# Decay attention with a two-of-four expert layer: multiplications and six gate operations from VectorE to GpSimd, in a new order

## The chip, the core and the metric

The kernel runs on one core of a Trainium2 chip. The metric is the device time of one execution in microseconds (us). A core has TensorE (PE, with its weight loads listed apart as PEld), VectorE (DVE), ScalarE (ACT), GpSimd (POOL) and the DMA queue of SyncE (SP). Each works through its own list of instructions in order, and semaphores tie the lists together.

## What is computed

Eight batches of 576 positions with 8 heads of 64 columns go through causal attention with a decay, and the result, turned to 576 x 512, through four attention "experts", of which each position takes the two with the largest gate logits:

```python
scores = scale * q @ k.T + cum[:, None] - cum[None, :]      # cum: running sum of log f, per head
attn   = softmax(where(causal, -1e9, scores)) @ v           # per batch and head
x      = attn.transpose(0, 2, 1, 3).reshape(B, S, H * D)
logits = x @ w_gate                                         # two of four experts per position
for e in range(E):
    a   = softmax(where(causal, -1e9, scale * (x @ wq[e]) @ (x @ wk[e]).T))
    ye  = a @ (x @ wv[e]) @ wo[e]
    out += gate[e] * ye                                     # gate: softmax of the two, else 0
```

## The kernel before

**Units.** Work is cut into pairs of heads. A batch has four pairs of kind "a" (attention) and two of kind "m" (experts): a3.2 is pair 2 of batch 3, m3.1 the second expert pair of batch 3. Each pair goes through `prep_attn` or `prep_moe` (the q and k operands, each split into a rounded part and a remainder), `max_pass` (row maxima, reduced by VectorE, L624 and L640), `scores` (score matmuls L716 and L717, exponentials on ScalarE, the triangular cuts L703 and L772 on GpSimd, and on GpSimd the additions L776, L778, L780 and L782 that fold a pair's blocks into `R` for the row sums), and `attend` (28 matmuls with the values, L801, and two copies of the output to `ot`).

**Row sums.** Two pairs share the rest. `row_sums` multiplies `R` with ones on TensorE (`sm`, L839), turns the sums (L854), takes reciprocals (for experts times the gates, L862), turns them back (L868) and spreads them over the partitions with two DMAs (`bt`, L874). `apply_rows` then takes each of the two pairs in turn: the output is multiplied by the spread reciprocals (L886, 128 x 576), ScalarE writes the rounded part (L905), and VectorE the remainder (L913). The rounded parts and remainders of a batch's four attention pairs are the operands of `moe_front` (values and gate logits, L439) and `prep_moe` (L544); those of its two expert pairs are the operands of `project_out` (`po`, L936), whose blocks go to the output.

**Gates.** After a batch's values, `moe_front` makes the gates from the logits in fifteen small operations on 80, 20 or 5 columns (L473 to L505), all of them on VectorE but one exponential on ScalarE (L494). 256 short matmuls in all, 32 for a batch, turn the gates (`pg`, L512), and two copies put them where `row_sums` of the expert pairs reads them.

**The order.** Every function is a generator which yields after each step. `ORDER` is a string in which two characters name a task; the kernel calls the next step of that task at each place. So the order of each engine's list is written out by hand in this string, and `SLOTS` names the buffer that each new tile takes. `NWARM` = 110 matmuls on zeros (L205) are one of the tasks, for the beginning.

Of the kernel before, what the change touches and what calls it, by code (L numbers as in the profile page):

```python
# [32 lines left out]
0e0e0e0e4z0e080303080h080e0e0e080808080h08080808080h08080h0e080e0e0j0j0j0o0t040e0j0j0j0e0e080808080808084w4w080e
0j0j0o0o0j0j0j0j0j0j0j0j0j0j0j0j0j0j0j0j0e0j0o0h0f0f0f0f0o0f0f0o0o0q0f09080j0t0j090f0f080f0f0f0f03080q0A0q0f0q0q
0q0j0j0q0f0f0f0f0q0q0t0q0k0k0k0A0q0k0q0d0f0f0q0k0t0k0k0k0a0t0t0k0a0a0a0a0f0q0F040k0k0k0q0k0q0k0f0k0q0q0f0k0q0i0k
0k0q0q4A0q0q0q0k0k0k0k0k0f0q0v0v0v0v0v0v0f0v0v0v0v0p0v0A0k0q0A0a0A0F0a0g0v0v0v0v0v0v4A0v0v0g0t0k0q0o0v0l0v0q0l0a
0q0q0B0t4y0a090C0C0v0v0v0v0v0C0g0C0C0C0C0C0C0C0C0r0r0r0r0r0r0r0r0b0f0r0r0r0r0r0C0C0C0r0v0v0v0v0C0C0C0r0r0r0r0C0C
# [1006 lines left out]
```

## Time and profile before

| | us |
|---|---|
| median of 3 runs (641.13 to 643.39) | 641.9 |
| profiled execution | 642.41 |
| span of the profiled execution | 640.7 |
| TensorE busy | 627.2 (98%) |
| VectorE busy | 541.1 (84%) |
| ScalarE busy | 481.9 (75%) |
| GpSimd busy | 409.7 (64%) |
| DMA: mean over 16 engines | 43.7% of the span |

Busy time counts an engine while an instruction runs, a VectorE instruction that stands still behind another engine included. Idle time of an engine matters only where TensorE ends up waiting for it. The granted TensorE clock is 1.00 of its full level, 2.4 GHz, in every stretch of the span but the last 0.7 us, which holds no work.

### The profile page before, as it was taken

What the parts mean: (1) busy time and instruction counts of PE and PEld (TensorE: products, weight loads), DVE (VectorE), ACT (ScalarE), POOL (GpSimd) and SP (SyncE); (2) the same over time, 40 slices, a digit from 0 to 9 for tenths busy, and PEclk for the clock granted to TensorE, in tenths of its full rate; (3) what the DMA queues carried; (4) which work ended last, traced back from release to release, by engine and by line L of the source; (5) the groups of instructions that cost most, each with busy time, mean ns of one, the idle gap of its engine ahead of it and who ended that gap; (6) DMA issues with size and microseconds to landing.
All of it is one profiled execution on the core that took longest, in us unless ns stands there. A gap on an engine that the chain in (4) does not pass through costs nothing.

```text
span 640.7 us, 15170 instructions
## 1 busy us (share of the span) xinstructions
PE 627.2 (98%) x5303; PEld 538.1 (84%) x5303; DVE 541.1 (84%) x1541; ACT 481.9 (75%) x1057; POOL 409.7 (64%) x519
## 2 busy tenths in 40 slices
PE   8899999999999999989999999999999999999997
PEld 6677889789888988869888898887987789879976
...
GB/s 195 154 168 194 136 55 143 137 90 96 141 140 130 80 158 144 161 55 62 170 145 66 148 174 40 139 142 83 119 105 136 134 109 76 79 98 21 107 70 202
DMA packets 33531, 76.90 MB, mean 120 GB/s; under 512 B 4395, under 2 KB 4875, under 8 KB 33455
## 3 DMA queue, kind: packets, MB, share of 16 engines
q1 hardware_dynamic: 33455, 75.94, 43.7%
...
## 4 chain that ended last, share of the span: by engine, by line
PE 88%; DVE 6%; issue 2%; DMA 2%; ACT 1%; SPq 1%; POOL 0%; DVEq 0%; POOLq 0%
PE pp_m L544 16%; PE ob_a L801 10%; PE pv L439 7%; PE po L936 7%; PE s_a L716 7%; PE s_a L717 7%; PE m_a L618 6%; PE m_m L618 4%; PE ob_m L801 4%; PE oa_a L801 4%; PE s_m L716 4%; PE s_m L717 4%; PE sm_a L839 3%; PE warm L205 2%; PE oa_m L801 1%
## 5 line engine op out<-in xcount | busy, mean ns | idle before, releaser
L703 POOL TENSOR_SCALAR_AFFINE_SELECT P_a<-P_a 128x256 f32<-128x256 f32 x128 | 65.3, 527 | 112.7 <-ACT P_a L734 67.2
L716 PE MATMUL s_a<-ka_a 128*128 128x320 f32 (+4 forms) x384 | 104.2, 296 | 1.1 <-DVE mxs_a L624 0.9
L717 PE MATMUL s_a<-kq 128*128 128x320 f32 (+4 forms) x384 | 102.9, 294 | 0.0
L624 DVE CUSTOM_DVE_ANT_0 junk_a<-m_a,mask 128x192 bf16<-128x192 f32 (+2 forms) x186 | 86.8, 486 | 17.3 <-PE m_a L618 15.4
L618 PE MATMUL m_a<-kq 128*128 128x448 f32 (+3 forms) x372 | 80.7, 304 | 4.0 <-DVE mxs_a L624 3.1
L552 ACT ACTIVATE kq<-pp_m 64x288 fp32r<-64x288 f32 x128 | 51.9, 406 | 31.6 <-PE pp_m L544 30.1
L716 PEld LDWEIGHTS s_a<-ka_a 128*128 128x128 f32 (+1 forms) x384 | 69.2, 180 | 4.4 <-DVE mxs_a L624 1.6
L717 PEld LDWEIGHTS s_a<-kq 128*128 128x128 f32 (+1 forms) x384 | 68.6, 180 | 1.2
L557 DVE TENSOR_TENSOR ka_m<-pp_m,kq 64x288 fp32r<-64x288 f32 x128 | 58.2, 454 | 12.9 <-ACT kq L552 9.7
L801 PE MATMUL ob_a<-P_a,va 128*64 128x320 f32 (+1 forms) x512 | 67.5, 406 | 0.0
L776 POOL TENSOR_TENSOR R_a<-P_a 128x896 f32<-128x896 f32 x32 | 67.5, 2110 | 0.1
L618 PEld LDWEIGHTS m_a<-kq 128*128 128x128 f32 (+1 forms) x372 | 57.6, 180 | 9.7 <-DVE mxs_a L624 4.4
L703 POOL TENSOR_SCALAR_AFFINE_SELECT P_m<-P_m 128x256 f32<-128x256 f32 x64 | 33.7, 543 | 48.2 <-ACT P_m L734 31.0
L778 POOL TENSOR_TENSOR R_a<-R_a,P_a 128x640 f32<-128x640 f32 x32 | 55.3, 1731 | 1.8
L801 PEld LDWEIGHTS ob_a<-P_a,va 128*64 128x64 f32 x512 | 35.8, 137 | 24.0
L716 PE MATMUL s_m<-ka_m 128*128 128x192 f32 (+2 forms) x192 | 51.8, 295 | 0.0
L717 PE MATMUL s_m<-kq 128*128 128x192 f32 (+2 forms) x192 | 50.9, 294 | 0.0
L624 DVE CUSTOM_DVE_ANT_0 junk_m<-m_m,mask 128x192 bf16<-128x192 f32 (+2 forms) x96 | 44.9, 485 | 5.3 <-PE m_m L618 4.3
L399 DVE TENSOR_TENSOR ka_a<-xin_a,ka_a 64x1152 fp32r<-64x1152 f32 x32 | 47.9, 1497 | 0.7
L734 ACT ACTIVATE P_a<-s_a 128x512 f32<-128x512 f32 x64 | 36.8, 598 | 13.2 <-PE s_a L717 12.0
L399 DVE TENSOR_TENSOR ka_a<-xin_a,kq 64x1152 fp32r<-64x1152 f32 x29 | 42.5, 1465 | 0.8
L618 PE MATMUL m_m<-kq 128*128 128x320 f32 (+3 forms) x192 | 41.2, 298 | 0.0
...
## 6 DMA issues: line engine op xcount, KB each, us to landing
...
```

What stands on the lines that cost most here:

```text
L399: eng.tensor_tensor(lo, x[at], hi.bitcast(F32), ALU.subtract)
L544: nc.tensor.matmul(pp[:, :HS], w[:, c, es], x[c][:, gs], start=(n == 0), stop=(n == 3 * KC - 1))
L552: nc.scalar.activation(hv[h], src[h], AF.Copy)
L557: nc.vector.tensor_tensor(lo[:, h, gs], src[h], hv[h].bitcast(F32), ALU.subtract)
L618: nc.tensor.matmul(dst, qB[0:K, h, i0 : i0 + dst.shape[0]], kB[0:K, h, j0:j1], start=True, stop=True)
L624: nc.vector.tensor_tensor_reduce(jk[:, :n], src, mask[:, MW - n :], 1.0, init, ALU.add, ALU.max, acc)
L703: return nc.gpsimd.affine_select(pv, pv, [[0, 2], [1, 128]], ALU.is_ge, 0.0, base=0, channel_multiplier=-1)
L716: nc.tensor.matmul(dst, kaf[:, c : c + m], qA[:, h, i0:i1], start=True, stop=False)
L717: nc.tensor.matmul(dst, kqf[0:K, c + h * S : c + h * S + m], qB[0:K, h, i0:i1], start=False, stop=True)
L776: g.tensor_tensor(r[:, :, 128:S], p[:, :, 320:768], p[:, :, 768:1216], ALU.add)
L778: g.tensor_tensor(r[:, :, 256:S], r[:, :, 256:S], p[:, :, 1216:1536], ALU.add)
L801: mm = nc.tensor.matmul(dst[64 * h : 64 * h + 64, c0 : c0 + rhs.shape[-1]], vs[h][0:kp, blk], rhs, start=first, stop=last,)
```

## The change

Two things are moved from VectorE to GpSimd: the multiplication by the reciprocals in `apply_rows` (48 of them), and six of the gate operations of each batch (48 in all). The sums, comparisons, maxima and reciprocals of the gates stay on VectorE. No instruction is added or left out, and no DMA.

```diff
 (moe_front)
-        nc.vector.tensor_tensor(g4, g4, up.unsqueeze(1).to_broadcast([128, 5, E, E]), ALU.mult)
+        nc.gpsimd.tensor_tensor(g4, g4, up.unsqueeze(1).to_broadcast([128, 5, E, E]), ALU.mult)
...
-        nc.vector.tensor_tensor(t4, t4, low.unsqueeze(1).to_broadcast([128, 5, E, E]), ALU.mult)
+        nc.gpsimd.tensor_tensor(t4, t4, low.unsqueeze(1).to_broadcast([128, 5, E, E]), ALU.mult)
...
-        nc.vector.tensor_tensor(g4, g4, t4, ALU.add)
+        nc.gpsimd.tensor_tensor(g4, g4, t4, ALU.add)
...
-        nc.vector.tensor_tensor(gt, lg, mx.unsqueeze(2).to_broadcast([128, 5, E]), ALU.subtract)
+        nc.gpsimd.tensor_tensor(gt, lg, mx.unsqueeze(2).to_broadcast([128, 5, E]), ALU.subtract)
...
-        nc.vector.tensor_tensor(gt, gt, wins, ALU.mult)
+        nc.gpsimd.tensor_tensor(gt, gt, wins, ALU.mult)
...
-        nc.vector.tensor_tensor(gt, gt, sm.unsqueeze(2).to_broadcast([128, 5, E]), ALU.mult)
+        nc.gpsimd.tensor_tensor(gt, gt, sm.unsqueeze(2).to_broadcast([128, 5, E]), ALU.mult)
 (apply_rows)
-            nc.vector.tensor_tensor(xf, grp["bt"][p], xf, ALU.mult)
+            nc.gpsimd.tensor_tensor(xf, grp["bt"][p], xf, ALU.mult)
```

The string `ORDER` is written anew from end to end, and five of the `SLOTS` lines with it (P, wide, banks, strips and some of the small ones); both orders have 4939 places and call the same steps. Three stretches of the two strings, read step by step:

- The beginning: of the 110 warm-up matmuls 85 stand ahead of the first matmul of the second maximum pass (a0.1) in the old order, 99 in the new one.
- Row sums to use: between the `sm` matmuls of a0.3 and the first matmul on rows that they scale stand 77 matmuls in the old order and 80 in the new; for a7.3 it is 91 and 101.
- The end: in both orders TensorE's list runs attend m7.0, attend m6.1, `sm` of m7.1, `pg` of batch 7, attend m7.1, and then 30 `po` matmuls ahead of the first `po` of batch 7. In the new order GpSimd's list ends with L776 to L782 of m7.1, L496 and L505 of batch 7, and the multiplications of batches 6 and 7.

## Rows read from the trace of the kernel before

**Rows 1.** The page's busy time, share of the span and instructions, by engine.

```profile
PE 627.2 (98%) x5303; PEld 538.1 (84%) x5303; DVE 541.1 (84%) x1541; ACT 481.9 (75%) x1057; POOL 409.7 (64%) x519
```

**Rows 2.** Stretches of 20 us: length, engines' busy us (instructions), clock, DMA share, GB/s.

```profile
0.00:20.00 20.00, 16.31 (x119) 12.97 (x119) 14.15 (x35) 15.47 (x19) 18.23 (x30) 1.00 0.59 192
20.00:40.00 20.00, 17.65 (x130) 14.13 (x128) 17.86 (x56) 17.09 (x31) 19.16 (x20) 1.00 0.55 159
...
260.00:280.00 20.00, 19.45 (x147) 16.08 (x145) 17.88 (x43) 17.26 (x37) 11.00 (x16) 1.00 0.54 152
280.00:300.00 20.00, 18.20 (x165) 16.64 (x166) 16.70 (x49) 12.75 (x30) 9.30 (x14) 1.00 0.21 61
...
420.00:440.00 20.00, 18.95 (x147) 15.43 (x144) 17.38 (x43) 17.21 (x40) 12.88 (x18) 1.00 0.51 149
...
sum 640.70, PE 627.20 PEld 538.14 DVE 541.12 ACT 481.87 POOL 409.68; mean PE 19.01 PEld 16.31 DVE 16.40 ACT 14.60 POOL 12.41
```

**Rows 3.** Timeline of 274 to 284 us: start, us, engine, instruction [idle before].

```profile
274.39 2.10 POOL L776 TENSOR_TENSOR R_m<-P_m 128x896 f32<-128x896 f32 x1
274.57 2.54 DVE L913 TENSOR_TENSOR xl_a<-ot_a,xh_a 128x576 fp32r<-128x576 f32 x1
...
276.57 1.94 POOL L778 TENSOR_TENSOR R_m<-R_m,P_m 128x640 f32<-128x640 f32 x1
277.04 2.09 DVE L886 TENSOR_TENSOR ot_a<-bt_a,ot_a 128x576 f32<-128x576 f32 x1
...
279.96 2.11 POOL L776 TENSOR_TENSOR R_m<-P_m 128x896 f32<-128x896 f32 x1
...
280.53 2.15 DVE L913 TENSOR_TENSOR xl_a<-ot_a,xh_a 128x576 fp32r<-128x576 f32 x1
280.66 0.39 PE L618 MATMUL m_a<-kq 128*128 128x256 f32 x1 [1.06 <-DVE mxs_a L624]
...
283.42 1.03 PE L618 MATMUL m_a<-kq 128*128 128x448 f32 x6 [1.14 <-DVE mxs_a L624]
```

**Rows 4.** Timeline of VectorE and GpSimd about 430 us.

```profile
430.15 3.83 DVE L886 TENSOR_TENSOR ot_a<-bt_a,ot_a 128x576 f32<-128x576 f32 x2 [0.47 <-DMA bt_a<-rr_a]
...
431.21 2.10 POOL L776 TENSOR_TENSOR R_m<-P_m 128x896 f32<-128x896 f32 x1
```

**Rows 5.** VectorE's groups by line: busy us, mean ns | idle before.

```profile
L886 DVE TENSOR_TENSOR ot_a<-bt_a,ot_a 128x576 f32<-128x576 f32 x32 | 28.9, 906 | 0.9 <-DMA bt_a<-rr_a 0.8
...
L886 DVE TENSOR_TENSOR ot_m<-bt_m,ot_m 128x576 f32<-128x576 f32 x16 | 12.1, 754 | 0.5 <-DMA bt_m<-rr_m 0.5
...
L505 DVE TENSOR_TENSOR gt<-gt,sm 128x20 f32<-128x20 f32 x8 | 3.2, 398 | 0.2
...
L479 DVE TENSOR_TENSOR t<-t,low 128x80 f32<-128x80 f32 x8 | 1.8, 225 | 0.0
```

**Rows 6.** One line each of GpSimd: least/median/longest ns, first to last start.

```profile
L778 POOL TENSOR_TENSOR R_a<-R_a,P_a x32: 1548/1568/2753, 30.4 to 560.7; 128x640 f32<-128x640 f32 x32
...
L780 POOL TENSOR_TENSOR R_a<-R_a,P_a x32: 995/1012/2166, 33.1 to 562.4; 128x384 f32<-128x384 f32 x32
...
L782 POOL TENSOR_TENSOR R_a<-R_a,pl x32: 447/454/1652, 47.3 to 563.5; 64x128 f32<-64x128 f32 x32
```

**Rows 7.** GpSimd's longest wait: who waited for whom, us in total, times, longest.

```profile
POOL P_a L703 <- ACT P_a L734: 67.2, 18, 9.1
```

**Rows 8.** Timeline of the end; the last row is from the chain that ended last.

```profile
617.46 0.45 POOL L782 TENSOR_TENSOR R_m<-R_m,pl 64x128 f32<-64x128 f32 x1
...
618.23 1.18 PE L839 MATMUL sm_m<-R_m,ones_col 128*32 128x288 f32 x16
...
625.73 0.76 DVE L886 TENSOR_TENSOR ot_m<-bt_m,ot_m 128x576 f32<-128x576 f32 x1 [0.50 <-DMA bt_m<-rr_m]
...
627.98 0.75 DVE L886 TENSOR_TENSOR ot_m<-bt_m,ot_m 128x576 f32<-128x576 f32 x1
...
622.53 14.52 PE po L936 x63
```

More of the change, by code (lines that the diff above doesn't have):

```diff
@@ L33 @@
[L33 to L37, printed above, removed]
@@ new lines @@
+4w4w4w4w4w4w4w4w01004w4w0000004w0202024z4w0c024w4w4w000202020202024w4w4w4w024w05054w0505020202020202024w4w02024w
+4w4z4w024z02020c0c024w020202024z070707030702020207074w054w4w0c0c07030307074w0705054y0c070c0707070707070707070707
+0h4w4w030303030e030303030303030303034w4z4z03030303030307070d07070e0e0707070h4z4z0h0e0e0e0h0e0e0e0e0e040e0c0e0c0e
+0e0e0e0e0e0e030h0e08080808080308080o080e0e08080h0e08080808080h080t08080e08080808080j0j0j0j0j0j0j0j0e030j0e0e0e0e
+4y044w0j4w0j4w4w0i0j0j0o0j0j0j0j0j0j0j0j0j0j0j0f0f0o0t090o0h090j0f0j0j0f0f0f0j0o0o0v0A0o0f0f080q0f0f0j080q0f0j0q
@@ new lines @@
+0q0f0q0f0f0q0q0f0f0f0f0t0f0q0q0q0q0f0f0k080q0q0q0q0k0k0q0f0q0q0q0q0q0f090q0q0q0k0k0k0k0k0a0k0t0t0A0a0a0k0q040k0k
+0k0k0k0k0k0k0q0q0t0a0p0k0k0k0k0k0F0A0v0v0A0f0a0a0k0v0v0v0v0v0A0C0k0v0v0v0a0F0g0v0f0v0v0v0v0v0v0v0v0v0v0q0v0q0q0g
+0k0o0f0l0l0t0v0C0C0C0C0C0v0C0C0t0g0r0r0r4A0r0r0r0r0r0r0r0C0a0a0C0r0r0r0v0v0v0r0b0r0C0C0C0C0C0C0C0C4A0r0C0C0C0r0r
+4A0F0m0m0m0m0r0m0b0v0v0r0r0C0w0m0m0C0l0F0C0w0w0w0w0w0r0b0F0b0m0b0b0b0b0w0A0b0w0w0w0w0s0w0m0s0s0M0C0H0b0n0H0w0w0w
+0w0w0H0H0H0H0H0w0H0C0C0H0N0H0H0M0C0R0R0N0n0C0n0R0n0H0H0n0n0n0n0H0u0w0n0H4y0O0H0H0N0M0H0H4A0R0H0H0H0H0N4A0w0w0H0r
@@ new lines @@
+0M0Y0A0R0H0r0N0H0r0r4A0A0N0C0N0N0N0N0N0N0N0N0N0N0N0N0N0N0N0N0N0N0w0M0N0N0N0N0N0N0N0N0N0N0D0D0D0D0D0D0D0D0D0D0D0D
+0D0N0N0O0M0O0O0D0D0D0D0D0F0H0H0F0F0H0O0D0D0x0I0I0D0G0x0Y0O0H0O0Y0O0O0O0M0M0D0M0M0M0x0n0Y0N0O0O0O0O0O0O0O0O0O0O0O
+0O0O0w0I0n0Y0I0I0w0w0I0w0I0I0I0I0I0I0O0O0I0Y0I0I0I0I0I0Y0y0Y0y0R0O0O0+0O0N0O0O0D0R0R0R0R0R0R0R0R0R0R0R0R0R0R0R0R
+0R0+0+0R0R0+0R0+0y0D0+180I0R0D0I0D0R0R0M0R0R0R0R0I0R0I0I0y0y0P0P0P0P0P0P0+0+0+0+0+0P0P0P0P0P0R0M0S0P0S0S0S0S0S0S
+0S0S0y0M0P0P0P0S0S110M0M0M0I0y0P0P0P0P0P0B0S0M0M0M0P0P0b0S0S0y0I0S0S0M0S110S110S0S0S0S0S0S0M0M0M0M0M0P0P0S0z0M0S
@@ new lines @@
+0R0R0R0+0+0+0+0+0M0M0M0M0M0M0+0+0+0+0S0I0M0J0+0+0+0M0S0z0J0E0E0E0K0+0S0K0K180+0+0M0K0y0T0P0S0T0T0T0T0T0T0T0T0T0T
+0T0T0T0T0T0T0T111111110+0K0+0T0T0T1313131d0Z0K0P0+13131313131313130+180Q0K181813120-0-1313131d0-0Q131313130K0J0-
+0T13130K130T0T0-130T0-13130-0-0-0-0-0-0-0-130Q0-180-0-0-0-0M131a1a0-0-1a1a1a1d1d1a0-1a130M181a1a1a0M0M0M0L0M0U13
+1a0M0z13111d0M0M0M0L100z1a0L0z101a0z0L0L0L0U0L1a1a1a1a1a1e1a1a1a1a0U14101f0z1414141414141414141f140z1a1a1a1a1f14
+0T141f1f1f141f1f1f1f141f141414141414140V0z0M0L0L1a1f1f1f1f1f1a1a0M0M1a141k0V0V1w0V1k1k1l1f1f1l1l181l1l1l1b1b1b1b
@@ new lines @@
+1414191b1b1b0L1d0-1b1b0V1f1f1f1f1f0V0L1f1f1d1p1p1p1p1k1k1p1b1b1b0V1b1b1b1b0V0V1b1b1b1b1b1b4A0V1f1l1l1f0-1m0-1f0z
+0z1l1l1l1l1l1l1l1l1l1p1f1l1l1l1l1l1l1l1l1l1l1l1l1l1l1d1p1p1B0-1b1p1b1p1p1p1p1p1p1p1p1p1l1l1k1k1k1k1k1k1q141l0W1l
+1m1m1p1l1m1p1p1p1m1m1p1p1p1g1p1m1p1p1p1p1p1p1p1m1q1p161m160W161m1m0W0W1g0W0W1g4A0W1q1f1g1g1g1g1q1q1p1q1q1q1q1k1k
+1k1k1k1k1k1p1g1q1q1p1b1g1g1g1g4A4A1g1g4A1m1m1m1m1m0W1m1m1m1q1q161q1g1g1g1g1g1g1m1m1g1g1g1g1g1l1l1m161q1q1q1q161m
+1m1m1I1w161k1q1w1w1w1w1w1B1w1q151c151h161h1p1m1m1m1q1h17151k1k1k1q0W1q1q1q1k1k1k171y1k1k1y1y1q1y1y1m1m1c1y1y1y1n
@@ new lines @@
+1y4A171q1k1k1g171q1b1n1n1n1n1y1y1k1n1n1n1n1n1n1n1n1k1n1n1n1x161k1C1y1y1y1y1y1y1y1n1y1y1n1i1717171n1n1n1B1y1y1y1y
+1k1y1n1i1i1i1q1i1r1q1r1r1r1r1r1r1r1r1r1r1r1r1r1r1r1r1r1r1r1r1r1B1B1B1N1B1i1k1k1r1r1r1i1i1i1D1y1o1y1J1D1r1D1D1D1D
+1o171I1I1I1n1D1o1D1D1D1D0X0X0X0X0X1k1D1D1k1D1N1y1k1k1y1I1D1D1D1D1D1D1D1D0X0X0X0X0X0X1B1y1D1D1D1D1k1k1n1s1D1k1D1k
+1K1c1k1D1K1K1z1z1z1z1z1z1z1k1k1s1s1K1K1K1K1z1z1z1z1K1K1D1K1E1E1z1z1n1K1z1z1z171U1z1z1K1K1K1V1K1K1K1K1z1K1K1E1n1P
+171K1t1t1t1k1N1N1N1j1V1E1j1j1j1V1k1K1K1K1j1j1j1j1j1E1U1U1E1E1V1E1E1K1K1E1E1E1E1k1U1t1t1E1E1E1E1E1K1U1K1U1K1K1E1V
@@ new lines @@
+1V2g1W1z1Z1I1Z1V1z1I1P1P1P1P1V1V1V1V1V1V1P1P1z1z1E1E1Z1I0X1Z0X1P1P1V1V1P1V1V1V1Z1z1z1Z1U1U1U1U1U1L1V1Z1L1L1L1L0X
+0X1P1N1P1P1V1t1P1V1P1N1E1L1L1L1L1L1E1V1P1P1P1P1P1P1P1P1P1P241t1L1V1V1V1V1E1V1V1V1V1V1V1V1V1V1V1P1z1L1L1L1L1L171L
+1E1E1L1P1t1P1L1L1L1Z1Z1+1L241U1U1U1t1Z1u1U1U1U1U1W1W1Z1W1W1W1W1W1W1P1P1W1U1Z1W1Z1Z1Z1Z1Z1Z1Z1Z1Z1Z1V1W1W1W1j1j1W
+1t1L1Z1Z1Z1Z1Z1Z1Z1Z1Z1Z1Z1Z1W1L1Z1Z1+1G1G1L1N1G1G1G1G1Z1Z1A1G1G1A0W0W1A1O1F1u1u1G1u1u1u1u1u1u1F1W1Q1Q1Q1Q1Q1W1Q
+1F291+1+1+1+1+1Q1Q1Q1Q1+1Q1+1+1Q1+1W1Q1Q1H1Q1Q1Q1Q1Q1Q1Q1W1W1V1Q1+241+1W1W1W1L1Q1W1H1+1+1W1+1+1+1+1U1U1U1U1U1U1U
@@ new lines @@
+1U1U1Q1Q1Q1u1u1U1U1+1+1+1+1W1+1W1W1U1+1+1U1U241H1H251W1R1M1H1H1H1H1S1S1S1R1+1X1R1X1X1X261+1H1S1M241+261S261X261S
+26261U1U1X1X1X1X1X1X1X1X1X1X1X261X1X2626261X1X1X261X1S1-1-1-1+1-2h1S2l1-1H29291v1v241M2429291v261v1v1v1v1v1v1v1v
+1v1X261X26262626261v1v1v2626261-1-1-1-1-1-26261-1-1S1T1U1U241U1U1v1v1-2a1-2626261v1-1U1-2b2b2b2b1v2b2b2b291T2b2b
+2b1X1-1-1-1-1U262g262b1-1Y1Y2g1v2l201Y1-1-2029262b2b262b2b2b1T2s2g2g1-2b27272727272b272027271X1T2i2b2b2b2b1T1T2b
+1-2b2b2b2727272i2i27272727271U1U1U1U1U27271T2b2t2b21211U211U2i2t2i2g2s2s2i2i2l1U292t2t2b1T2b2c2c2c2c2c1T2c2c2c2c
@@ new lines @@
+2c212l1T2c2c2c2c2c2c2c2s2c272c1T2l2s27271H2i272l2l2s2s2s2s2s2i2i2s2s2s2n27212n21212i2n2n2n2n2n2s2s2s2s2n2n2n2n1v
+2i212s2s2s2s2s2s2s2c4y4y2i2t2i272c2c2c2c2s212i2i2i212s2i2s2n2n2t2t2t2t2E2t2n2n2n2n2n2i2i2n2n2t2t2s2n2n2n2n2n2n2t
+2t2t2t2i2i2i2i2i2t2t2t2t272c272i2t2t2t2t2t2t2t2t2t2t2t2t2i2i2i2i2t2t2t2n2n28282n222g2t222c2n2l2x222g22222222222d
+2m2t2e2o2e2e2d2o282e2j2j2e2s2s2s2s2s2u2u2u2s2s2o2e2e2j2j2j2j2u2o2o2s2u2o2o2u2u2u2o2o2s2u2j2j2j2j2u2u2s2j2j2j2j2j
+2s2e2o2o2o2u2u2u2t2u2s2s2s2o2u2o2o2o2o2j2u2j2u2u2222222u2u2f2s2y2o2d2j2j2E2j2o2J2o2o2E2E2j2o2u2j2u2E2o2o2x2E2E2e
@@ new lines @@
+2u2j2u2o2o2j2x2j2x2x2x2x2x2x2x2x2x2x2x2x2x2x2x2x2x2x2x2x2x2x2x2x2x2x2x2x2x2x2x2x2x2s2y2s2f2k2u2u2u2u2u2k2y2y2y2y
+2y2f2f2f2k2J2y2y2E2y2p2y2y2F2y2y2y2y2y2y2y2y2y2v2f2G2G2v2v2y2y2y2j2K2G2G2v2v2v2v2v2v2y2y2v2v2v2f2G2v2G2G2G2G2G2G
+2v2v2v2v2v2v2v2v2v2v2y2p232G2G2G2G2x2x2G2G2y232G2G2G2G2f2J2q2q232G2f2G2Q2q2q2Q2y2z2z2y2z2z2z2z2z2z2z2G2z2z2z2z2z
+2z2q2z2z2z2z2z2z2z2z2z2G2G2z2G2G2Q2w2v2L2v2w2S232J2J2J2J2L2L2L2L2L2L2L2J2L2L2q2s2G2H2H2p2323232G2L2q2L2H2L2L2L2L
+2L2L2L2H2L2L2L2L2L2Q2Q2V2q2q2H23232L2L2w2S2S2z2S2S2S2H2H2S2S2H2H232S2S2H2H2H2S232Q2H2H2H2H2H2v2H2H2H2H2L2L2L2S2L
@@ new lines @@
+23232S2S23232r2S2S2S2S2X2S2S2S2S2A2V2V2S2r2r2r2V2V2B2s2A2A2V2s2B2B2B2B2r2r2r2r2r2r2M31302M2S2M2M2M2M2M2M2M2M2S2H
+2H2M2M2M302M2M2M2M2M2M2H2S2S2Q2X2X2X2X2X2X2X2X2s2X3h2H2Q313131323131312X2B3131313030312X2X30302B312M2M3c2X2X2X31
+312M2M312M2M2M3131313131313131312X2X2X2X312B2X3131313131312S2S2S2X2X2X2X2X3130303131313031303030303030303132312T
+2T2T2T2T3032322T302V2H2T2T2T2T2T2T2T2T2T2T2T2V303030302B2B3232323232322T2T2C2C30302C2C2C2C2X2O2X2X2X2C2C3c3c2O2O
+2f2O3c3c2O3o2O322N3c3c3c2I2I2I2R2O2N2N2O2Y2Y2Y2Y3232323232323232322T0X2T3e32352T2T2Y2Y2Y2T2Y32322Y35352Y353e2Y2W
@@ new lines @@
+2Y2Y3e3e322Y2Y352Y2Y2Y2Y2Y2Y2Y2Y3232322Y3e3e32323e3e3e3e3e2C3h35353535353535353535353535353535353535353535353535
+3535352f322C2r3e2C3e3e3e2P3e2D30303e3e3030303030302D2D303033333335353535333333333333332P2T3333363636333333363636
+363636353333363e3333333e3e3e3e2U3e2O3h362D36333o3h3e2Y3e363636362Y332T3636363636363636363h2+2D2+342U2+2+3e2+3336
+363e2Z36362P362+2+2+2U343334372Z2P373j2P2P2P3j3j3h3e2P2P3e2Z37373j3j3j3j3030303030373737373737373j3j3j3j2D2P3t37
+3737303737303h3j3j2-3j3j3j3j3j3j30373j37372+37373o3737303030303h2D2-2P3j3j3j3o3f3f3f3f3f3f3f3o3f3f372D3j383j2-3j
@@ new lines @@
+373t3j383j2-2D2D2D2D3q383q3q3q3q3q3q3q3q3f3f3f3f3f2D2-3q3q3A3A3A3f3f3f3q3q3q3q3q3j3q3q3j3q3f3f33333739392-303030
+3t39392-3q3q3k3q3k2-3k3k3k3k3k2-3q3q3k3k3k2-3v3k3k3k3k3A3A3q3q3B39393t3t3t3k3k3k3k3A393q3k3k3k3p3B3q3q3B3o3o3o3B
+3B3B3q3v3v3v3f3f3f3f3B3B3F3F3B3B3v3v3v3v3v3v3v3A3A3A3B3B3B3B3k3k3B3M3B3B3B3B3B3B3B3B3B3r3r3B3B3B3B3B3B3B3r3r3r3r
+3B3B3B3B2-3v3v3v3v3v3d393A3A3A3F3F3F3r3C3r3r3r3C3r3r3r3v3k3v3v3v3v3v3v3v39393A3A3v3A3A3v3r3f3r3r3r3r4y3v3k3k3F3r
+3r3C3C3C3C3A3A3F3F3v3v3G3f3f3t3t3C3C3r3C3A3A3A3A3A3A3C3C3F3B3B3B3F3F3F3F3F3F3F3F3F3F3F3F3F3F3F3F3F3F3F3F3F3F3r3F
@@ new lines @@
+3F3F3F3F3r3r3r3r3i3v3C3A3A3A3A3A3A3C3C3a3C3C3F3C3A3C3C3A3a3a3a3a3A3A3M3G3A3C3C3C3C3m3m3m3g3l3l3g3l3a3Y3G3G3G3G3G
+3G3G3w3G3G3F3A3A3g3C3C3C3w3m3a3a3a3w3w3w3w3w3w3w3w3w3w3w3w3w3w3w3a3G3G3G3G3G3G3G3w3C3R3A3w3w3w3b3G3G3G3C3C3C3M3M
+3R3s3s3A3w3w3A3D3D3M3M3M3M3D3A3A3D3D3D3D3D3D3D3D3D3D3S3G3G3u3b3b3G3m3O3D3D3G3w3O3O3O3O3O3G3O3O3O3w3A3D3D3w3O3G3D
+3O3G3x3x3b3G3y3y3y3R3D3s3D3O3O3O3G3R3m3y3Y3y3D3R3O3D413O3D3H3H3H3O3O3O3O3O3O3O3m3H3m3a3m3D3O3H3H3H3H3H3H3H3H3H3H
+3b3b3b3O3T3T3T3T3T3T3T3T3T3T2D3y2D2D3H3H3H3H2D3H3H3H3O3O3O2D3R3O2D3T3A3T3H3T3T3T3T3T3T3T3T3T3T3+3Y413A3Y3Y3E3E3Z
@@ new lines @@
+3n3n3n3n3n3n3n3I3E3I3I3O3y3+3P3P3P3P3P3H3H3H3R3H3P3T3+3T3T3P3P3b3P3P3+3+3n3n3n3b3b3T3y2D3y3+3+3b3b3+3P3P3P3P3P3P
+3P3+3x3+3T3T3P3N3D3D3P3P3b3P3P3+3+3+3A3+3z3+3+3+3+3+3+3+3+3R3J3z3A3Q3J3Q3T3U3T3z3z3z3z3z3z3U3U3U3U3A493A3Q3J3z3z
+493Y3+3+3U3U3+493+3U3U3U3U3U3Y483U3U413U413Y3U3U3J41413J3J3J493J3U3U3U3+3+3P493+494949494949494949483U4949494849
+494949494949493U3J3U49494949494949494348433-49434349434349493-41413+4848484848484848484848484848484d433K3n43434d
+433K4d4848484d4843433-4343484343434343434343434343433K3U4a4d4d3b3b3b3-3P3P3P3-3-3-3-3-3-3-3-3-3-3-3-4a4a4a4a4a4a
@@ new lines @@
+4a4a4a3-3-3-3-4d4a4d434d4d4d4d4d4d3-484d3z494a434a43434a4a3U483U4a4a4d4d4d4d484e4a4d3-4d4d4d4d484d4d4d4d4d4d4d48
+4a4a3K4a4a48484a48443-4d4d4d4d44443-3-4444444e444444444444424a44444e3-4a4e44444a444444484a443W4a3W3W3W3W4a4m444d
+44444444443W3W4a3V3V3V3W3W233J4e4b4b4b4b4b4b4b4b4b4b4b4b4b4e4b4e4e4e4b4e4b4b4b4b4645404e464646464b4b4546464d3X3X
+3X3X3X3X45404b4c403X3X3X4c484l4e464e4l474p4k464k47474p4747474p47474e474e4e4k4e4e4e4e4e4e4e4e4e4l4l4k3K3K3K4k4p4l
+4l3K3K4e4l4l4l4l4l4l4l4l4l4l4e4p4e4d4p484p4p4l4l4l4l4848484l4p4p4p4p4l4l4l4l4p4p4p4p4p4k3X3X48484p4l484l4l4l4l4l
@@ L116 @@
+4t3L4s4t4i4i4i4i4i4i4i4i4i4i4s4i4t3L3L4j4j4j4j4j4j4j4u4u4j4u4u4u4j4j4j4j4u4j4j4u4u4u4u4u4j4j4v4v4v4v4v4v4v4v4v4v
 4v4v4v4v4v4v4v4v4v4v4v
@@ L122 @@
[L122 to L125 removed]
+P 01201201201021021020120210210120102101201202102012
```

105 lines of the change are left out of this document (14 added, 91 removed).

## The prediction

> **What bounds the kernel now.** I read the page's busy times first: TensorE is busy 98% of the span, VectorE 84% and GpSimd 64% [rows 1]. No matmul is added or taken away, so what the change can move is TensorE's idle time, 640.70 - 627.20 = 13.50 us [rows 2]. The second view cuts the span into stretches of 20 us, and in each the reader takes TensorE's busy time from the length. The first two stretches lack 3.69 + 2.35 = 6.04 us. Three stretches of the middle lack 0.55 + 1.80 + 1.05 = 3.40 us, while the others there lack next to nothing. The last projections run without a gap until 637.05, 3.65 us ahead of the end of the span, in which the last block is copied and stored [rows 8]; 0.41 us lies scattered. The start has no multiplication and no gate in it, and the last 3.65 us neither. So the change acts on the 3.40 us of the middle, and on whatever new idle time it makes.
>
> The third view is the timeline of those stretches. There TensorE waits 1.06 and 1.14 us for a reduction of VectorE, and VectorE was late because three of its instructions took far longer than the 0.75 us that they take alone: the remainder L913 2.54 and 2.15 us, and the multiplication L886 2.09 us. Each of them began while an addition of GpSimd was running and ended shortly after that addition [rows 3]. About 430 us two multiplications took 3.83 us instead of 1.5, again across an addition of 2.10 us [rows 4]. So a VectorE instruction with two large operands in the on-chip memory stands still until GpSimd's addition ends. The Trainium skill says so too, SBUF — State Buffer, "Who interferes with whom": a VectorE instruction with two SBUF inputs and a GpSimd instruction that reads SBUF shut each other out for a whole instruction. What that rule makes of the moved work is the second case below.
>
> **The change part by part.** *Taken from VectorE:* the multiplications, 28.9 + 12.1 = 41.0 us, and six gate rows, of which the largest and the smallest are shown, 14.2 us together [rows 5]. VectorE's busy time goes from 541.1 to 485.9 us, 76% of the span. In that is the time that the multiplications stood still: 2.09 - 0.75 = 1.34 us in the first bad stretch and 3.83 - 1.50 = 2.33 us in the second [rows 3, 4]. The second has no other cause, so it goes. In the first, the two L913 that stood still for 1.79 and 1.40 us stay on VectorE; but with 1.34 us and the multiplication's own 0.75 us gone, the reductions behind them start 2.1 us sooner, which is more than either wait of TensorE there.
>
> *Put on GpSimd:* its additions take 1.012 us for 384 columns and 1.568 us for 640 [rows 6], so 576 columns take 1.012 + 192/256 x 0.556 = 1.43 us, and 48 of them 68.6 us. A small operation lies on the line through 128 columns (0.454 us) and 384: 0.35 us for 80 columns and 0.22 for 20, 8 x (3 x 0.35 + 3 x 0.22) = 13.7 us. GpSimd goes from 409.7 to 492.0 us, 77%. That lies beside other work as long as GpSimd runs ahead: its longest single kind of wait is 67.2 us for exponentials [rows 7], as much as all multiplications. The Trainium skill speaks against the move, GPSIMD Engine Reference, "Engine selection": elementwise work with two inputs belongs on VectorE, GpSimd takes about twice as long. The rows agree (1.43 against 0.75 us). An estimate from the table in its section "Elementwise — side-by-side cycle accounting" (4497 ns for 2048 columns) would be 1.26 us for a multiplication and 60.7 us in all; the sum of the time is the same by either, because neither price lies on the path.
>
> *The chain of one pair:* the output is ready 0.68 us later per multiplication, but the two of a group now run back to back on GpSimd, where before VectorE's list held the second one until the first one's remainder was written (625.73 and 627.98, though the second takes only 0.75 us) [rows 8]. First pair +0.68 us, second pair 625.73 + 2 x 1.43 = 628.59 against 628.73 before. In the order the matmuls between the row sums and the first use are as many as before or more (80 for 77, 101 for 91), each worth 0.1 to 0.2 us, so this is covered. At the end the same 30 projections stand ahead of batch 7's, and I cost it at nothing; if the cover is short it is 0.68 us, once.
>
> *The added wait:* GpSimd now waits for the `bt` transfer. Behind a waiting multiplication in its list stand triangular cuts and additions, and for these wait the attend and row-sum matmuls. Likewise `pg` of the last batch now waits for L496 and L505 behind the last addition on GpSimd, with three VectorE operations between them: about 0.22 + 0.6 + 0.22 us after 617.91, while the row-sum matmuls hold TensorE from 618.23 for 1.18 us [rows 8]. That is covered by about 0.4 us if GpSimd is no later than before; each microsecond that it is later goes straight into the time. I take nothing, with 1.3 us (three operations of 80 columns and one of 20 in front of it) as the other end.
>
> *The new order:* nothing in the trace prices it. In the first 40 us, 14 more warm-ups stand early; the bounds are a gain and a loss of 1.0 us (a sixth of the 6.04 us), and I take zero, since the stretch's own instructions are the same. The order is for other durations, and it can hold new collisions: from none to as much idle time as before, 3.40 us. I take one of the size of a single wait, 1.1 us [rows 3], as the collisions' victims lose 48 large instructions and VectorE has 55 us more to make up for one.
>
> *Sum:* 642.41 - 3.40 + 1.1 = 640.1 us for the profiled execution, which lay 0.5 us above the median of the runs; for the median 639.6 us.
>
> **The rivals.**
> 1. *The collisions come back.* GpSimd is at work 77 / 64 = 1.2 times as much, and a remainder (L913) or operand split of VectorE finds a multiplication in its way where it found none. For it speaks that the two L913 show this victim already [rows 3], and that a group's second multiplication runs on GpSimd just while its first remainder is due on VectorE. Against it: VectorE is 8 points less loaded. Three waits of 1.1 us for the three removed: 642.0, within 0.3% either way. By the skill's rule named above the multiplications are readers like the additions, which is this case.
> 2. *GpSimd's list is late: slower.* A multiplication that waits for its transfer as long as VectorE did (0.50 us) and then takes 1.43 us puts 1.93 us in front of the cuts or additions behind it. Where GpSimd has no lead, attend or the row sums come 1.93 us late, and TensorE stops. Two such places (3.9 us) only return the 3.40 us; from three on, 5.8 - 3.4 = 2.4 us are lost: 644.3. For it: GpSimd was busy 18 to 19 of 20 us in the first two stretches [rows 2] and takes no later work out of turn. Against it: the order was made with the multiplications on GpSimd, and TensorE's waits in the middle name VectorE [rows 3].
> 3. *The beginning or the end decides.* A start 1.0 us better with no new collision gives 641.9 - 3.4 - 1.0 = 637.5, and with the scattered 0.4 us 637.1; a worse one with the end's 0.68 and 1.3 us gives 641.9 - 2.3 + 1.0 + 2.0 = 642.6.
>
> **How the numbers follow.** The forecast (VectorE relieved, one new collision or none) gets 0.46, the collisions come back 0.30, GpSimd late 0.16, beginning or end 0.08, half of it better and half within 0.3%. A measurement of this kernel can tell 0.3% (1.9 us) from no change. So faster 0.46 + 0.04 = 0.50; same 0.30 + 0.04 = 0.34; slower 0.16. The range runs from the best beginning, 637.0, to GpSimd late at three places, 644.3.
>
> **What would show it.** Right: L886 stands on GpSimd at about 1.4 us, VectorE's busy time is near 486 us and GpSimd's near 492, and the idle time of TensorE in the middle falls below 1.5 us. The first rival shows as L913 or L399 of 2 us and more across a multiplication, with TensorE waiting for VectorE's reductions; the second as TensorE waiting for L703, L772 or L782 of GpSimd, or `pg` for L505. The prediction is wrong if TensorE's matmuls themselves take another time than 627 us, or if the first 40 us change by more than 1 us.

## The result: 648.6 us, 1.1% slower

The changed kernel takes 648.6 us (median of 3 runs, 648.55 to 651.13) against 641.9; the ratio is 1.011 with a 95% interval of 1.0085 to 1.013. The forecast was 639.6 us, and 648.6 lies outside the range. The profiled execution is the one of 651.13 us, with a span of 649.1 us; the other two had spans of 646.5 us. So a stall that is read below may be larger there than in the median run: e12 (below), the same kernel with four warm-up matmuls less and a span of 646.3 us, lacks 0.50 us where 1.98 are read here, and has one stretch at the lower clock where two are read here.

What the move itself was to do it did. The page's busy line after, which answers to [rows 1], and GpSimd's multiplications (least, median and longest ns, first and last start):

```profile
PE 630.7 (97%) x5303; PEld 542.0 (83%) x5303; DVE 523.8 (81%) x1445; ACT 479.3 (74%) x1057; POOL 490.9 (76%) x615
...
L886 POOL TENSOR_TENSOR ot_a<-bt_a,ot_a x32: 1400/1422/1840, 63.8 to 581.3; 128x576 f32<-128x576 f32 x32
L886 POOL TENSOR_TENSOR ot_m<-bt_m,ot_m x16: 1396/1420/1936, 168.8 to 636.1; 128x576 f32<-128x576 f32 x16
```

A multiplication takes 1.42 us (1.43 was worked out) and GpSimd is busy for 490.9 us (492.0). But VectorE fell only to 523.8 us, not to 485.9, and TensorE is idle for 649.1 - 630.7 = 18.4 us where it was 13.5 [rows 2]. Its idle time by stretches of 20 us (length, then busy us of PE, PEld, DVE, ACT and POOL, granted clock, DMA share, GB/s), and two short stretches within the third and fourth:

```profile
0.00:20.00 20.00, 16.05 (x118) 12.57 (x119) 13.75 (x33) 15.06 (x19) 18.67 (x30) 1.00 0.62 201
20.00:40.00 20.00, 17.71 (x130) 14.30 (x131) 17.20 (x58) 17.59 (x31) 18.95 (x19) 1.00 0.63 171
100.00:120.00 20.00, 15.43 (x107) 14.43 (x107) 19.24 (x45) 10.56 (x23) 13.93 (x17) 0.91 0.42 121
160.00:180.00 20.00, 18.02 (x133) 16.94 (x132) 14.25 (x38) 12.06 (x30) 14.36 (x17) 0.91 0.70 160
280.00:300.00 20.00, 20.00 (x197) 16.66 (x196) 18.01 (x49) 17.11 (x34) 15.12 (x21) 1.00 0.43 117
420.00:440.00 20.00, 20.00 (x176) 15.17 (x176) 16.81 (x56) 13.71 (x33) 13.17 (x22) 1.00 0.47 110
500.00:520.00 20.00, 18.64 (x153) 14.71 (x150) 17.50 (x40) 13.21 (x28) 13.81 (x17) 1.00 0.51 139
...
103.60:107.00 3.40, 3.40 (x16) 3.40 (x15) 3.27 (x9) 1.56 (x4) 1.44 (x4) 0.50 0.89 355
175.20:178.70 3.50, 3.50 (x19) 3.50 (x18) 1.23 (x4) 0.77 (x2) 2.58 (x4) 0.51 0.40 105
```

The waits of the three stretches in [rows 2] are gone: 280 to 300 and 420 to 440 us are full now, and 260 to 280 too. In their place 4.57 us are missing at 100, 1.98 at 160 and 1.36 at 500. The beginning lacks 6.24 us (6.04 before) and the end 3.73 (3.65): both as forecast. Twice TensorE ran at its lower level, 1.2 GHz, for about 3.4 us, which adds, by an estimate from these two rows (half of each stretch), some 1.7 us of matmul time each: together 3.4, beside the 3.5 us by which its busy time grew. The kernel before had no such stretch in its profiled execution.

The timeline of the worst stretch (start, us, engine, instruction, idle before it and what ended that):

```profile
95.44 0.76 POOL L703 TENSOR_SCALAR_AFFINE_SELECT P_a<-P_a 128x256 f32<-128x256 f32 x2
95.90 3.63 DVE L399 TENSOR_TENSOR ka_a<-xin_a,kq 64x1152 fp32r<-64x1152 f32 x1
96.15 0.09 POOL L614 MEMSET mxs_a<- 64x2 f32 x1
96.22 2.10 POOL L776 TENSOR_TENSOR R_a<-P_a 128x896 f32<-128x896 f32 x1
98.39 2.56 POOL L778 TENSOR_TENSOR R_a<-R_a,P_a 128x640 f32<-128x640 f32 x1
99.56 2.61 DVE L399 TENSOR_TENSOR ka_a<-xin_a,ka_a 64x1152 fp32r<-64x1152 f32 x1
102.10 0.47 DVE L854 STREAM_TRANSPOSE zt_a<-sm_a 128x288 f32<-128x288 f32 x1
102.62 0.36 PE L618 MATMUL m_a<-kq 128*128 128x192 f32 x1 [1.74 <-DVE zt_a L854]
...
106.39 2.12 POOL L776 TENSOR_TENSOR R_a<-P_a 128x896 f32<-128x896 f32 x1
106.61 4.18 DVE L857 TENSOR_SCALAR rc_a<-zt_a 128x18 f32<-128x18 f32 x1
108.46 0.77 POOL L703 TENSOR_SCALAR_AFFINE_SELECT P_m<-P_m 128x256 f32<-128x256 f32 x2
109.17 0.11 POOL L614 MEMSET mxs_m<- 64x2 f32 x1
109.23 1.54 POOL L778 TENSOR_TENSOR R_a<-R_a,P_a 128x640 f32<-128x640 f32 x1
110.83 0.27 DVE L859 RECIPROCAL rc_a<-rc_a 128x18 f32<-128x18 f32 x1
111.96 0.53 PE L618 MATMUL m_m<-kq 128*128 128x192 f32 x2 [2.60 <-DVE mxt_a L640]
```

Two operand splits L399 stood across additions (L776 and L778), and TensorE waited 1.74 us for a transposition behind them. Then L857, which adds 1e-9 to 18 row sums, took 4.18 us: it began just after L776 and ended with L778, so five instructions of GpSimd went past it. TensorE waited 2.60 us for a reduction behind it. All three of these met additions; no moved multiplication is in this picture.

How L857 fared in the two kernels (least, median, longest ns), before first:

```profile
L857 DVE TENSOR_SCALAR rc_a<-zt_a x16: 170/178/358, 50.5 to 566.9; 128x18 f32<-128x18 f32 x16
L857 DVE TENSOR_SCALAR rc_m<-zt_m x8: 170/178/345, 145.9 to 620.0; 128x18 f32<-128x18 f32 x8
```

```profile
L857 DVE TENSOR_SCALAR rc_a<-zt_a x16: 164/179/4183, 53.1 to 573.1; 128x18 f32<-128x18 f32 x16
L857 DVE TENSOR_SCALAR rc_m<-zt_m x8: 163/220/1627, 152.5 to 629.0; 128x18 f32<-128x18 f32 x8
...
502.46 2.34 DVE L857 TENSOR_SCALAR rc_a<-zt_a 128x18 f32<-128x18 f32 x1
502.66 2.10 POOL L776 TENSOR_TENSOR R_m<-P_m 128x896 f32<-128x896 f32 x1
505.64 0.47 PE L716 MATMUL s_m<-ka_m 128*128 128x448 f32 x1 [1.35 <-DVE mxs_a L624]
...
572.90 1.41 POOL L886 TENSOR_TENSOR ot_a<-bt_a,ot_a 128x576 f32<-128x576 f32 x1
573.13 1.21 DVE L857 TENSOR_SCALAR rc_a<-zt_a 128x18 f32<-128x18 f32 x1
```

The same small instruction never took more than 0.36 us before. In the new order it stands across additions five times (4.18, 2.34, 2.02, 1.63 and 0.39 us) and across a moved multiplication once (1.21 us). At 502.46 us the addition began 0.20 us after it, while the triangular cut L772 was still running.

### The profile page after: what moved, and what is told of

Its sections match the earlier page's. It is cut to its first block, busy times and chain, and to the rows that moved or that the text cites. A ratio compares the mean times of both kernels' runs of the same rounds, so it can differ in the third digit from the quotient of the medians.

```text
span 649.1 us, 15185 instructions
## 1 busy us (share of the span) xinstructions
PE 630.7 (97%) x5303; PEld 542.0 (83%) x5303; DVE 523.8 (81%) x1445; ACT 479.3 (74%) x1057; POOL 490.9 (76%) x615
## 4 chain that ended last, share of the span: by engine, by line
PE 89%; DVE 4%; POOL 3%; DMA 2%; ACT 1%; issue 1%; SPq 0%; POOLq 0%; ACTq 0%; DVEq 0%
PE pp_m L544 15%; PE ob_a L801 10%; PE po L936 8%; PE s_a L716 7%; PE s_a L717 7%; PE m_a L618 7%; PE pv L439 7%; PE ob_m L801 5%; PE m_m L618 4%; PE s_m L716 4%; PE oa_a L801 4%; PE s_m L717 4%; PE sm_a L839 3%; PE oa_m L801 2%; PE sm_m L839 1%; DMA kq<-ms_a 1%
## 5 line engine op out<-in xcount | busy, mean ns | idle before, releaser
L703 POOL TENSOR_SCALAR_AFFINE_SELECT P_a<-P_a 128x256 f32<-128x256 f32 x128 | 66.7, 539 | 53.9 <-ACT P_a L734 32.4
L618 PE MATMUL m_a<-kq 128*128 128x448 f32 (+3 forms) x372 | 75.9, 302 | 3.5 <-DVE zt_a L854 1.7
L776 POOL TENSOR_TENSOR R_a<-P_a 128x896 f32<-128x896 f32 x32 | 68.5, 2141 | 0.0
L778 POOL TENSOR_TENSOR R_a<-R_a,P_a 128x640 f32<-128x640 f32 x32 | 53.2, 1665 | 1.4
L399 DVE TENSOR_TENSOR ka_a<-xin_a,ka_a 64x1152 fp32r<-64x1152 f32 x32 | 53.3, 1664 | 0.8
L703 POOL TENSOR_SCALAR_AFFINE_SELECT P_m<-P_m 128x256 f32<-128x256 f32 x64 | 30.5, 492 | 28.9 <-ACT P_m L734 14.2
L886 POOL TENSOR_TENSOR ot_a<-bt_a,ot_a 128x576 f32<-128x576 f32 x32 | 45.9, 1441 | 7.1 <-DMA bt_a<-rr_a 4.8
L399 DVE TENSOR_TENSOR ka_a<-xin_a,kq 64x1152 fp32r<-64x1152 f32 x29 | 47.8, 1649 | 0.8
```

The lines of the kernel that those rows point to most:

```text
L399: eng.tensor_tensor(lo, x[at], hi.bitcast(F32), ALU.subtract)
L618: nc.tensor.matmul(dst, qB[0:K, h, i0 : i0 + dst.shape[0]], kB[0:K, h, j0:j1], start=True, stop=True)
L703: return nc.gpsimd.affine_select(pv, pv, [[0, 2], [1, 128]], ALU.is_ge, 0.0, base=0, channel_multiplier=-1)
L776: g.tensor_tensor(r[:, :, 128:S], p[:, :, 320:768], p[:, :, 768:1216], ALU.add)
L778: g.tensor_tensor(r[:, :, 256:S], r[:, :, 256:S], p[:, :, 1216:1536], ALU.add)
```

## The experiments

Each run's time is given as its ratio to the kernel before, measured on the same chip beside it, with the 95% interval.

### The parts one at a time

First I asked whether the move costs the time or the order. Three kernels: the new order with every operation back on VectorE (e1), the old order with all of them on GpSimd (e2), and the new order with the multiplications alone back (e3), which is this line:

```diff
-            nc.gpsimd.tensor_tensor(xf, grp["bt"][p], xf, ALU.mult)
+            nc.vector.tensor_tensor(xf, grp["bt"][p], xf, ALU.mult)
```

> The new order and buffer slots, with the multiplications and the six gate operations all back on VectorE: the order alone. Theory A (the moved work itself costs, because it makes GpSimd hold up VectorE more often): near the kernel before, 641 to 644 us. Theory B (the order costs: it puts operand splits L399 and the small L857 beside GpSimd's additions, whoever multiplies): 647 us or more, since VectorE then has 55 us more to do in an order made without them, and the waits of TensorE at 102, 112 and 505 us stay.

> The old order and slots, with the multiplications and the six gate operations on GpSimd: the move alone. Theory A: slower than before by most of the 6.7 us, 646 to 649 us. Theory B: within 0.5% of before, 639 to 644 us, with the waits of TensorE at 280, 283 and 436 us shorter or gone, since the multiplications that stood still there are no longer VectorE's.

> The new order with the 48 multiplications back on VectorE and the gates left on GpSimd. Theory A: most of the loss goes with the multiplications (68.6 of the 82 us moved), 642 to 644 us. Theory B: no better than the changed kernel, 648 us or more.

Measured: e1 688.2 us (ratio 1.070, 1.065 to 1.076), e2 690.5 us (1.074, 1.069 to 1.079) and e3 678.5 us (1.057, 1.052 to 1.062). Neither part is near either kernel. TensorE's longest waits, with the new order alone (who waited for whom: us in total, times, longest):

```profile
PE m_m L618 <- DVE mxs_m L624: 5.7, 3, 2.8
PE m_a L618 <- DVE mxs_a L624: 4.1, 7, 1.2
```

and with the moves alone:

```profile
PE sm_m L839 <- POOL R_m L782: 7.6, 1, 7.6
PE m_a L618 <- DVE mxs_a L624: 3.3, 4, 1.4
```

Each order is made for its own placement: without the new one GpSimd's additions come late for the row sums (the second rival's mechanism, 7.6 us in one place), and without the move VectorE is late in the new order. So a part by itself doesn't show what that part costs in the pair, and all three runs miss both theories. What they leave is that the loss of the pair is small, 6.7 us, beside the 36 to 49 us of a mismatch, and has to be sought in single places of the trace.

### Another engine for the small addition

```diff
-        nc.vector.tensor_scalar(rc, zt[:, :, 0], 1.0e-9, None, ALU.add)
+        nc.scalar.activation(rc, zt[:, :, 0], AF.Copy, bias=1.0e-9)
```

> The changed kernel with one small operation elsewhere: the addition of 1e-9 to the row sums (L857, 18 columns, 24 of them) on ScalarE instead of VectorE, where single ones took 4.18 and 2.34 us. If these two are what TensorE waited for at 112 and 505 us (2.60 and 1.35 us), the time falls by 3 to 4 us and, where the drop of the clock goes with them, by up to 5.7: 643 to 645.5 us. If the wait only passes to the next instruction of VectorE with two operands or a fast copy mode, it falls by less than 1.5 us.

Measured (e5): 650.9 us (ratio 1.013, 1.007 to 1.019), no gain. In the stretch of 80 to 120 us the wait of 2.60 us went (TensorE busy for 38.26 us against 35.43), and the one of 1.35 us at 505 too, but others came elsewhere:

```profile
80.00:120.00 40.00, 38.26 (x311) 33.47 (x311) 36.12 (x88) 29.92 (x68) 35.36 (x42) 1.00 0.42 106
...
234.80 0.47 PE L716 MATMUL s_a<-ka_a 128*128 128x448 f32 x1 [1.51 <-DVE mxs_a L624]
```

This edit adds to ScalarE's list and puts two hand-overs between engines where VectorE had gone straight on, so by itself it does not clear L857. TensorE is idle for 16.5 us in it, and its busy time is 631.7 us with the clock at its full level up to 640 us; where these 4.5 us over the kernel before come from stays open, and they show that busy time can grow without the lower clock.

### One stall at a time

The next four take away the cause of a stall and add nothing to any engine. The first two move steps in the order, shown here as the steps that the places of the string name; the third edits the source; the fourth does all three.

```diff
 max_pass a2.3: first transfer of ms
+max_pass a2.3: second transfer of ms
 prep_moe m1.0: L557
...
 max_pass m1.1: L618
-max_pass a2.3: second transfer of ms
 scores a2.3: L716, L717
```

```diff
-prep_attn a2.0: second L399
 row_sums a1.1: L839
-prep_attn a2.0: L401
 row_sums a1.1: first L854
+prep_attn a2.0: second L399
+prep_attn a2.0: L401
```

```diff
-        nc.vector.tensor_scalar(rc, zt[:, :, 0], 1.0e-9, None, ALU.add)
         yield
-        nc.vector.reciprocal(rc, rc)
+        nc.vector.reciprocal(rc, zt[:, :, 0])
```

> The changed kernel with one step placed elsewhere in the order: the second half of the row maxima of a2.3 is sent out right behind the first half, not eight microseconds of TensorE work later. Theory S (each stall costs its own length, and the fall of the clock behind it): TensorE's wait of 1.98 us for this transfer at 174.7 us goes, and with it the 3.4 us at the lower clock level behind it, worth 1.7 us: 648.6 - 2.0 - 1.7 = 644.9 us. Theory L (a removed stall lets the lists meet otherwise, and another takes its place): within 1.0 us of 648.6, with the wait gone and a new one later.

> The changed kernel with one step placed elsewhere: the second operand split L399 of a2.0 (2.61 us at 99.6 us, against an addition of GpSimd) stands behind the first transposition L854 of the row sums of a1.1 instead of in front of it. Theory S: TensorE's wait of 1.74 us for L854 at 102.6 us goes and with it the 3.4 us at the lower clock level (1.7 us): 648.6 - 1.7 - 1.7 = 645.2 us. Theory L: within 1.0 us of 648.6, another wait within the next 20 us.

> The changed kernel with the small addition L857 (1e-9 onto the row sums, 18 columns) left out; the reciprocal reads the transposed sums itself. The 1e-9 is the part of the computation that is missing. Theory S: the addition's 4.18 us at 106.6 us and 2.34 us at 502.5 us go, and TensorE's waits of 2.60 and 1.35 us behind them: 648.6 - 4.0 = 644.6 us. Rival V: what stood still was the place in the list, not the instruction; the reciprocal L859, now the first at that place, stands across the same instructions of GpSimd for 2 to 4 us, and the time stays within 1.0 us of 648.6.

> All three edits in one kernel: the early second transfer, the swapped operand split, and no addition of 1e-9 (that part of the computation is missing). Theory S: the four long waits (1.98, 1.74, 2.60 and 1.35 us) and the two stretches at the lower clock (1.7 us each) go: 648.6 - 11.1 = 637.5 us, less than the kernel before (641.9). Theory L: at least half of it comes back as new waits: 643 us or more.

Measured: e6 648.2 us (ratio 1.010, 1.008 to 1.013), e7 647.2 us (1.008, 1.006 to 1.011), e8 642.2 us (1.0004, 0.9988 to 1.0019), e9 642.2 us (1.0002, 0.9987 to 1.0018).

The early transfer (e6) looks as theory L said: the wait at 174 us is gone, and at 343 us a new one stands:

```profile
343.52 1.02 PE L618 MATMUL m_m<-kq 128*128 128x256 f32 x6 [1.42 <-DVE mxs_m L624]
```

But theory S had priced a wait that is large in one execution: at 160 to 180 us e7 and e12, in which this step is not moved, lack only 0.23 and 0.50 us, at the full clock. So e6 does not decide between the two.

The swapped split (e7) brings 1.4 us of the 3.4 that theory S asked, and the intervals of e7 and of the changed kernel overlap. The 1.74 us wait falls apart into 0.49, 0.26 and 0.38 us, the one behind L857 stays (1.90 us), and so does the lower clock (0.91 in 100 to 120 us).

Leaving the small addition out (e8) brings 6.4 us, more than its two waits (4.0 us), and the changed kernel is then as fast as the one before. Its stretches, and behind them one of e12, which still has L857:

```profile
100.00:120.00 20.00, 18.27 (x147) 15.57 (x147) 19.00 (x54) 11.72 (x27) 17.66 (x23) 1.00 0.54 145
160.00:180.00 20.00, 19.83 (x169) 17.30 (x170) 17.45 (x53) 15.26 (x30) 15.19 (x17) 1.00 0.55 150
500.00:520.00 20.00, 20.00 (x193) 16.04 (x193) 16.78 (x45) 15.65 (x36) 16.71 (x22) 1.00 0.55 149
...
160.00:180.00 20.00, 19.50 (x156) 18.33 (x154) 17.11 (x51) 14.98 (x38) 15.14 (x19) 1.00 0.64 160
```

At 100 us 2.84 us come back, at 500 us 1.36. At 160 us 1.81 come back too, although nothing was edited there; most of that belongs to the one profiled execution, since e12 lacks only 0.50 us there with L857 in place. Both stretches at the lower clock are gone. The rival V (whatever stands at that place stands still) falls. The reciprocal, now first in line with 18 columns and one operand, takes what it always takes, while additions run (the profile's lines here are one lower):

```profile
L858 DVE RECIPROCAL rc_a<-zt_a x16: 249/267/268, 53.3 to 564.5; 128x18 f32<-128x18 f32 x16
...
105.90 2.10 POOL L776 TENSOR_TENSOR R_a<-P_a 128x896 f32<-128x896 f32 x1
106.86 0.27 DVE L858 RECIPROCAL rc_a<-zt_a 128x18 f32<-128x18 f32 x1
```

So it is the form of L857 that stands still, not its place and not its size. The Trainium skill, SBUF — State Buffer, "Who interferes with whom", names `tensor_scalar` among the operations that can take the port pair that VectorE shares with GpSimd, by two-port modes, and says that the pair is held for a whole instruction while the other engine blocks fully. L857's rows agree, but at 106.61 us it stood through five instructions of GpSimd and not one, so the measurement goes beyond that rule; in which mode L857 ran, no run here shows.

All three together (e9) are no faster than e8, between what the two theories say. In the profiled execution the waits at 100 us are down to 0.47, 0.26 and 0.38 us, but a stretch at the lower clock came back there:

```profile
106.20:109.70 3.50, 3.50 (x14) 3.33 (x15) 2.24 (x8) 1.99 (x4) 2.89 (x5) 0.51 0.45 178
```

That stretch is not what holds e9 at the time of e8: ten of its twelve runs have a granted clock of 1.00 over the whole run, and their median is 641.7 us. What does, stays open. What brings the clock down is not settled by these runs either: e8 as profiled had a single wait of 1.73 us there and kept the full level, e9 as profiled had only short waits and lost it, and in most of its runs e9 kept it.

### Controls: the kernel before, and a shifted start

Does leaving the small addition out help any order? And does a time belong to the order, or to the instants at which two lists happen to meet? e10 is the kernel before with the edit of e8. e11, e12 and e13 are the kernel before, the changed one and e8, each with

```diff
-NWARM = 110
+NWARM = 106
```

> The kernel before with the small addition L857 left out (the 1e-9 on the row sums is the part that is missing), as a control: in the kernel before none of its 24 instances took over 0.36 us. Theory C (the addition costs only where it meets one of GpSimd's additions): within 1.0 us of the kernel before, 641.9 us. Rival G (24 instructions less on VectorE's list help any order): about 6 us faster, as they did in the changed kernel, so near 636 us.

> The kernel before with 106 warm-up matmuls instead of 110, 0.57 us less of TensorE's work at the start, and nothing else changed. Theory F (a time belongs to the order and the placement): 641.3 to 641.9 us. Theory P (it belongs to the exact instants at which the lists of VectorE and GpSimd meet, and a shift deals them anew): 1.5 us or more away from 641.9, with other waits in the middle.

> The changed kernel with 106 warm-up matmuls instead of 110, and nothing else changed. Theory F: 648.0 to 648.6 us. Theory P: 1.5 us or more away from 648.6, in either direction, with the small addition L857 standing still at other places.

> The changed kernel without the small addition (the 1e-9 is missing) and with 106 warm-up matmuls. Theory F: within 0.6 us of the 642.2 us that it takes with 110. Theory P: 1.5 us or more away from 642.2.

Measured: e10 643.9 us (ratio 1.0004, 0.997 to 1.004), e11 642.5 us (0.9965, 0.993 to 0.9995), e12 648.7 us (1.0071, 1.004 to 1.010), e13 643.3 us (0.9996, 0.997 to 1.0025). Leaving L857 out of the kernel before gains nothing clear of the interval, which is 2.3 us wide to either side; rival G's 6 us are excluded. So the 6.4 us go with where the new order puts L857.

With 106 warm-ups no kernel's median moved by more than 1.2 us, short of the 1.5 of theory P. The ratios of e11 and e12 lie lower than those with 110, because the runs of the kernel before beside them took 643.8 us in the mean, against 642.3 beside e6 to e9. In e12 the long waits are the old ones, but for the transfer at 174 us, of which 0.50 is left:

```profile
PE m_m L618 <- DVE mxt_a L640: 2.8, 1, 2.8
PE m_a L618 <- DVE mxs_a L624: 1.9, 3, 1.1
PE m_a L618 <- DVE zt_a L854: 1.7, 1, 1.7
PE s_m L716 <- DVE mxs_a L624: 1.4, 1, 1.4
```

So the stalls of L857 come back in another execution, at the same additions (3.42 us at 106.46, 2.34 at 499.63). Theory P was hardly put to the test: four warm-ups less hardly shifted the lists, since by then L857 begins at 106.46 us in e12 against 106.61, and in e11 at 96.39 against 96.30. e12 and e13 differ by L857 alone and give its price a second time: spans of 646.3 and 640.9 us, 5.4 us apart.

## Why the prediction was wrong

Its first steps held. The multiplications cost 1.42 us on GpSimd and lie beside other work; GpSimd's busy time was right within 1.1 us. The waits of the three stretches went. The beginning lacks 0.2 us more and the end 0.1; the sum had nothing for either, with bounds of 1.0 us for the beginning and of 0.68 and 1.3 for the end. Rival 2 (GpSimd's list late) did not happen with the new order: no long wait of TensorE names GpSimd. It did happen with the old one (e2).

The step that failed is the term "The new order": one new collision of 1.1 us, bounded by the 3.40 us of before. The new order put 4.57 + 1.98 + 1.36 us of idle time into the middle, with 0.50 at 40 to 60 us 8.4 us, and the lower clock added 3.4 by the estimate above. In e12, whose span is that of the median run, it is 4.53 + 0.50 + 1.35 + 0.39 = 6.8 us and one stretch at the lower clock: still six times the 1.1 us. Three things in it were wrong.

First, the victims. I drew from [rows 3, 4] that an instruction "with two large operands" stands still, and counted 48 victims fewer. A victim with one small operand, L857, was not on the list, and it caused most of the 6.7 us: 6.4 by e8, with e10 as the control, and 5.4 by e12 and e13. The trace of before shows it, in small: four times L857 began there in the last 0.08 to 0.31 us of an addition, and where most was left it took twice its 0.18 us and ended with the first of the two additions in this row:

```profile
454.04 3.11 POOL L778 TENSOR_TENSOR R_a<-R_a,P_a 128x640 f32<-128x640 f32 x2
455.31 0.34 DVE L857 TENSOR_SCALAR rc_m<-zt_m 128x18 f32<-128x18 f32 x1
```

The section of the Trainium skill that the prediction cites for two-operand instructions names `tensor_scalar` a few lines on. Read to the end, it would have put 24 more possible victims into the count.

Second, the relief. VectorE was to fall by 55 us and fell by 17. Part of the missing 38 us is time stood still. By the groups of lines, L399 takes 53.3 + 47.8 us instead of 47.9 + 42.5, L857 12.3 + 3.2 instead of 3.4 + 1.6, and L913 29.7 + 14.1 + 5.1 instead of 27.2 + 11.6 + 5.0: 26.3 us more in all. Other lines took 4.0 us more, most of it in the gate operations L473 and L486, which met moved multiplications and an addition. The last 7.6 us are no work: VectorE's groups add up to 616.9 us before and 592.0 after, while its busy time, 541.1 and 523.8, counts once what runs at the same time. So the 55.2 us of the moved groups could not come off the busy time whole. The two groups of L399 after (busy us, mean ns | idle before):

```profile
L399 DVE TENSOR_TENSOR ka_a<-xin_a,ka_a 64x1152 fp32r<-64x1152 f32 x32 | 53.3, 1664 | 0.8
L399 DVE TENSOR_TENSOR ka_a<-xin_a,kq 64x1152 fp32r<-64x1152 f32 x29 | 47.8, 1649 | 0.8
```

Third, the size of what follows. A stall was priced at its own length. L857's two waits are 4.0 us, its price 6.4 (e8) and 5.4 (e12 against e13). Between e12 and e13 the sum is plain: 2.80 us of idle time at 100 us and 1.22 at 500, 0.53 less at 160, and 2.0 us more of TensorE's busy time, with one stretch at the lower clock in e12 and none in e13.

Without the accident the forecast would still have been 2.6 us too low: e8 takes 642.2 us. There the three old waits are gone (3.40 us), but 1.73 us are missing at 100 us behind the two L399, 0.39 at 40 and 0.17 at 160, and TensorE's busy time is 0.9 us longer. So the first rival, collisions that come back (its sum gives 641.8 us, not 642.0), was right in the main for all but L857: 2.3 us for the 3.4 of before, most of it at L399 and the transposition behind it. But what TensorE waited for stood across additions, not across multiplications as the rival had it. L913 and gate operations did meet moved multiplications (L913 took up to 1.40 us, L473 1.28), and TensorE did not wait there. What VectorE was spared bought no time, since TensorE had waited for it in three stretches of the middle only, and the new order made other waits.
